# A feature-map attention block beside a Mish MLP on one core: a new order of all steps, first loads split anew over two queues, numerators over 64 rows

## The chip, the cores and the metric

One core of a Trainium2 chip. The time is that of one execution of the whole program on the device, in microseconds, lower is better. The kernel before took 151.50, 151.67 and 151.73 us in three runs, median 151.67.

## The reference, cut to what matters

All inputs are bf16; S = 2048 tokens, D = 448, 16 heads of 28, F = 1792.

```python
xn  = layernorm(x)                                # (1, 2048, 448)
q, k, v = heads(xn @ wqkv)                        # 16 heads of 28
phi(t) = concat(softmax(t @ w_phi), softmax(-(t @ w_phi)))   # per head, 56 wide
kv  = phi(k)^T @ v ;  z = sum over tokens of phi(k)
o   = (phi(q) @ kv) / (phi(q) @ z + 1e-6)
out = x + o @ wo + mish(xn @ w1 + b1) @ w2
```

## The kernel before, in words

The 2048 tokens are 16 tiles t of 128 and 8 units u of two tiles. Everything stays in SBUF; products go to the eight PSUM banks, which are taken in pairs. The program is a list of steps by name (`ORDER`). Each step issues instructions to one or more engines, and every engine works off its own instructions in the order of the list, waiting on semaphores only. So the list sets the order of all five engines and of both DMA queues (SP's and ACT's), and also which pair of banks a step gets: the pair that has lain unused longest.

The steps, by name (a last letter d, a, p, s or m says DVE, ACT, POOL, SP's queue or a transposing DMA; A, B, E, O, H are parts of a product over the 448 input rows):

- `lx6.8` loads tiles 6 and 7 of x. `lkm`, `lvm`: the first 384 rows of the key and value weights (tile `Wkv`). `lkt`: their last 64 rows, twice, "the tails". `lp`: w_phi into `Wbd`, four small loads. `lqT0` to `lqT3`: the query weights by transposing DMAs (`WqT`, L312). `lb`: b1. `l1m`, `l1t`, `l2.0` to `l2.3`, `lo`: W1, W2, wo.
- `zN`: N products of zeros, 128 by 512, whose result nobody reads (L406).
- `st`, `rs` or `rp`, `xn`: mean and variance of a tile, its reciprocal deviation, the normalized tile. `xtUm` transposes a unit of it by a DMA on SP's queue; `xt3E`, `xt3O` do it for unit 3 on PE (L514).
- `wtk0`, `wtk1`: PE transposes the key weights (L548), a copy goes to `Eq`. `wmk0`, `wmk1`: PE multiplies them by `Wbd` (L572), the copy is `Wpk`. `qd`: DVE doubles the last rows of `WqT` (L316). `wmq0`, `wmq1`: the same product for the query weights, the copy is `Wpq`.
- `kU`, `qU`, `vU`: the products of a unit of xn with `Wpk`, `Wpq` and the value weights, 14 products over 64 rows each (parts A, B, H) or 6 over 128 rows and 2 over 64 (E, O, H). When the last part is done, ACT takes two exponentials of k or q (L613, L679), and ACT or DVE copies v (L519, L521). All the products of these steps and of `f` are on line L441.
- `kn`: DVE sums and inverts (L621, L623), and POOL or DVE multiplies (L625). `kvU`: PE adds the unit to the one sum over tokens (L643). `kvz` writes it out and transposes it by a DMA into `KVZ`.
- `eT`: transposing DMA of the exponentials of q, tile t (`EqT`).
- `fQ.C`: the first MLP product for half Q of the tokens and chunk C of F; ACT applies Mish (L698).
- `ndT`: numerators and denominators of tile t, 16 products over 56 rows (L721), then six DVE instructions. `otU`: transposing DMA of the result.
- `gT`, `woU`: the second MLP product and the product with wo (L825, L842), added in one bank; DVE adds x (L790); `sto`, `stt` store. The last tile is stored in two parts, on ACT's and SP's queue.

Of the kernel before, what the change touches and what calls it, by code (L numbers as in the profile page):

```python
# [14 lines left out]
DH = 28  # L15
# [5 lines left out]
G = 4  # L21
# [17 lines left out]
class Program:  # L39
# [13 lines left out]
    def op(self, eng, fn, r=(), w=(), dma=False, tag="", after=()):  # L53
        o = Op()
        o.tag, o.parts = tag, None
        o.eng, o.fn, o.dma, o.needed, o.count, o.sem = eng, fn, dma, False, 0, None
        o.idx = len(self.ops[eng])
        deps = list(after)
        for res in list(r) + list(w):
            if res[0] == "ps":  # L60
                deps += [a for e, a in self.psum.get(res, {}).items() if e != eng]
        for res in r:
            if res[0] != "ps":
                deps += self.writers.get(res, [])
# [74 lines left out]
class Banks:  # L139
# [37 lines left out]


ORDER = """
zero pwd lkms lx6.8a table z14 ph lx4.6s pv lkta lpa st7d st4a st6d lx2.4s st5d pi pe wtk0d rp6p pp2 rp4p xn7a lbs lqT0 xn6d lqT2 b1 wtk1a  # L180
st2d xt3Ed lqT1 xn4d xt3Od lqT3 wmk0a xn5d wmk1a pp0 pk qd st3d v3Ha rp2p lvms wmq0d lx8.12s xn2d wmq1a st9a xn3d lx0.2s st11d v3Aa xt2m k3A
q3H st10d lx12.16s q3A st8d st0d rp10p xt1m rp8p st14d pp1 v3Ba q3B xn9d k3B v2Ha st15d xn10d xn8d st1d v2Aa q2B k3H v2Ba xn11d st13d q2H
rp14p rp0p k2B q2A l1ts k2A v1Bd xn14d xn15d st12d k2H k1H rp12p v1Ad k1B e6 xt4m v1Hd q1B ep k1A xt5m xt7m q1A k4B q1H v4Aa xn12d v4Ha k4A
xn13d k4H k5H xt6m k5A v4Ba xn0d e7 k5B xn1d xt0m e2 v5Ad l1ms v5Hd k7H kn2.1p kn1.0p k7A kn4.1p v5Bd kn4.0p k7B kn7.0p kn3.1p kn5.1p k6H
kn1.1p k6A q6B k6B q6H k0A q6A k0H v6Ha v6Aa k0B e3 q4B v6Ba v7Ba e5 q4A v7Ha v7Aa kn5.0p v0Ad e12 e4 e13 v0Hd kn7.1p kn3.0p f0.2H q4H v0Bd
f0.2B f0.3B f0.2A f0.3H f0.0A kn6.1p f0.0H f0.3A kn6.0p kn0.0p q5H f0.0B q0B q5A e8 kv4 kv1 f0.7H q5B f0.7A q0A kn2.0d q0H f0.7B kv5 kv7 kv6
f1.12H f1.12A f1.7A kn0.1d f1.12B f1.7B kv2 kv3 kv0 f0.12B e11 kvz e1 f1.11H f1.11A f1.7H f0.12A f0.12H f1.11B f0.8A f1.0B l2.0s f0.6B f0.9B
e9 f0.6A f1.0H f0.6H f0.8H f1.0A f0.9H f0.9A f0.10A f0.8B e10 f0.10B nd3 f0.10H f0.13B f1.10A f1.10H f0.13A f0.13H l2.3s f1.10B nd4 q7B
f1.8B q7A q7H f1.5B nd7 f1.8A f1.8H f1.5H f1.5A l2.2s f1.1H f1.1A los e0 f1.3A f1.1B f1.3B f1.9B nd1 f1.3H f1.9H f1.9A f0.11B f0.1A nd2
f0.1H f1.13A f0.1B f1.13B f0.11H f1.6H f1.13H f0.11A nd5 f1.6A f0.4H l2.1a e15 e14 f0.4A f1.6B f0.5B wob nd0 f0.4B f1.4B f0.5A f0.5H f1.2B  # L190
f1.4H ot1m f1.4A wo1H nd6 f1.2H f1.2A wo1B ot2m ot0m ot3m nd12 wo1A nd10 nd15 g3 g0 g2 g1 nd9 wo3B nd8 wo3H wo0B wo3A wo0H wo0A ot4m nd14 g6
g8 g7 wo4H ot7m wo2B nd13 sto0 wo4A nd11 sto3 wo4B g5 g9 g4 g10 ot5m ot6m wo5H wo7B wo5A wo6A wo2H wo2A wo7A wo7H wo6H wo5B wo6B sto1 g14
sto2 g11 g13 g12 sto4 sto6 stt14 sto5 g15 stt15
"""


# [5 lines left out]
def _kernel(es, nc, A_x, A_wqkv, A_w_phi, A_wo, B_w1, B_b1, B_w2, out):  # L202
    def sb(name, shape, dtype):
        return es.enter_context(nc.sbuf_tensor(name, shape, dtype))
# [37 lines left out]
    EqT = sb("EqT", [P, NT, 2 * G, P], BF16)  # L242
# [3 lines left out]
    KVZ = sb("KVZ", [P, 2 * G, P], BF16)  # L246
# [33 lines left out]
    def bank(b, n=1):  # L280
        return PS[:, b * TCW:(b + n) * TCW]
# [10 lines left out]
    def pb(b):  # L292
        return ("ps", b)
# [122 lines left out]
    def pe(fn, r, w, tag, after=()):  # L416
        return op("PE", fn, r=r, w=w, tag=tag, after=after)
# [295 lines left out]
    def nd(t):  # L713
        b = take2(False)

        def f(e):
            for s in range(2):
                for g in range(G):
                    for r in range(2):
                        at = (s * G + g) * NDW  # L720
                        ins = e.matmul(  # L721
                            bank(b + r)[:, at:at + NDW], EqT[64 * r:64 * r + QP, t, s * G + g, :],
                            KVZ[64 * r:64 * r + QP, 2 * g + s, 64 * r:64 * r + 64].rearrange("p (b c) -> p b c", b=2)[:, :, 0:DH + 2],
                            start=True, stop=True)
# [260 lines left out]
```

## Time and profile before

| What | Value |
|---|---|
| median of three runs | 151.67 us (151.50 to 151.73) |
| the profiled execution | 151.33 us, of which 149.0 us are span |
| busy in the span | PE 144.7, DVE 102.3, ACT 77.1, POOL 34.1 us |
| the fourteen zero products (L406) | 0.88 to 6.96 us |
| PE without a gap | from 12.00 to 146.07 us |
| one `st` step on ACT (L472, L474, L476) | 0.58 + 0.19 + 0.20 + 0.67 + 0.19 = 1.83 us |
| granted TensorE clock | 1.00 in all stages |

The span begins with the first instruction of the program and ends with the last; 2.33 us of the execution lie outside it. A row of the trace reads: start in us, length in us, engine, line, operation, what it writes and reads. A small q after an engine's name (SPq, ACTq) marks the issue of a transfer, and the time is that of the issue; the landing comes later. Matmuls overlap, so the distance between starts is what counts for them.

### The profile page before, as it was taken

The page shows a single profiled execution, that of the slowest core. Times are in us where ns is not written, and L with a number is a line of the kernel's source. Part 1 is how long each engine was busy: PE and PEld are TensorE (multiplying, and loading weights), DVE is VectorE, ACT ScalarE, POOL GpSimd, SP SyncE. Part 2 cuts the span into 40 slices and gives each one's busy share as a digit, 9 for nine tenths or more (in the row PEclk, how much of TensorE's full clock was granted, in tenths as well). Part 3 has the DMA queues.
Part 4 walks back from the last instruction along what each step waited for, and adds up shares of the span by engine and source line. Part 5 has one row for each costly group of instructions (what it writes and reads, how often), then busy time and mean ns, then how long its engine had stood idle before and what let it go on. Part 6 is the DMA issues. An engine that isn't in the chain of part 4 may idle for free.

```text
span 149.0 us, 3836 instructions
## 1 busy us (share of the span) xinstructions
PE 144.7 (97%) x1664; PEld 77.0 (52%) x1664; DVE 102.3 (69%) x214; ACT 77.1 (52%) x90; POOL 34.1 (23%) x46
## 2 busy tenths in 40 slices
PE   7979999999999999999999999999999999999993
PEld 2456555555445554445555556555554555665552
DVE  0699799999999940048939897997998891041222
ACT  3389999999899969587995776000000000000000
POOL 3233552599999900000000000000000000000000
PEclk9999999999999999999999999999999999999999
DMA  4999985689993305999250392200011507020005
GB/s 102 285 198 313 191 165 128 141 163 298 211 175 78 75 4 115 205 288 235 60 122 0 75 176 66 62 0 0 7 37 39 174 0 185 0 105 22 0 1 183
DMA packets 40980, 17.46 MB, mean 117 GB/s; under 512 B 34948, under 2 KB 40196, under 8 KB 40964
## 3 DMA queue, kind: packets, MB, share of 16 engines
q1 hardware_dynamic: 39484, 16.18, 49.4%
q10 hardware_dynamic: 1480, 1.04, 3.5%
q8 instruction: 13, 0.21, 0.6%
q14 instruction: 3, 0.02, 0.0%
HBM read 7.02 MB, written 1.84 MB: 59 GB/s over the span
## 4 chain that ended last, share of the span: by engine, by line
PE 96%; ACT 1%; DVE 1%; issue 0%; POOL 0%; POOLq 0%
PE PS L441 50%; PE PS L825 28%; PE PS L842 7%; PE PS L406 4%; PE PS L721 2%; PE PS L643 2%; PE PS L572 1%; ACT xn L504 1%; ACT Eq L519 1%; DVE Eq L521 0%; DVE x_all L790 0%; PE PS L548 0%; DVE x_all L811 0%; POOL zeros L363 0%; DVE shift L499 0%
## 5 line engine op out<-in xcount | busy, mean ns | idle before, releaser
L441 PE MATMUL PS<-xnT,W 64*128 64x512 bf16 x392 | 45.4, 376 | 0.0
L825 PE MATMUL PS<-W,actT 128*128 128x448 bf16 (+1 forms) x224 | 42.7, 351 | 0.0
L698 ACT ACTIVATE actT<-PS,b1T 128x1024 bf16<-128x1024 f32 x28 | 29.7, 1114 | 7.4 <-PE PS L441 7.4
L825 PEld LDWEIGHTS PS<-W,actT 128*128 128x128 bf16 x224 | 21.6, 98 | 20.2 <-issue 0.7
L441 PEld LDWEIGHTS PS<-xnT,W 64*128 64x128 bf16 x392 | 19.4, 94 | 20.0 <-ACT actT L698 0.8
L625 POOL TENSOR_TENSOR actT<-actT,rSk 128x896 bf16<-128x896 bf16 x14 | 24.1, 1760 | 3.3 <-DVE rSk L623 3.3
L790 DVE TENSOR_TENSOR x_all<-PS,x_all 128x448 bf16<-128x448 f32 (+1 forms) x16 | 9.6, 617 | 19.0 <-PE PS L825 11.3
L621 DVE TENSOR_REDUCE Sk<-actT 128x32 f32<-128x896 bf16 x16 | 16.6, 1039 | 0.0
L613 ACT ACTIVATE actT<-PS 128x896 bf16<-128x896 f32 x16 | 14.0, 941 | 0.5 <-PE PS L441 0.2
L441 PE MATMUL PS<-Wpq,xnT 64*128 64x448 bf16 x112 | 14.0, 349 | 0.0
L441 PE MATMUL PS<-Wpk,xnT 64*128 64x448 bf16 x112 | 13.5, 349 | 0.0
L441 PE MATMUL PS<-Wkv,xnT 64*128 64x448 bf16 x112 | 13.3, 350 | 0.0
L737 DVE COPY Sq<-PS 128x32 f32<-128x32 f32 x16 | 3.0, 188 | 14.8 <-PE PS L721 14.8
L480 DVE BATCH_NORM_STATS2 stats<-x_all 128x6 f32<-128x448 bf16 x14 | 8.6, 614 | 3.9 <-DMA x_all<-in_A_x_dram 3.9
L746 DVE TENSOR_TENSOR v_all<-v_all 128x464 f32<-128x464 f32 x16 | 10.3, 642 | 0.6
L742 DVE TENSOR_TENSOR v_all<-PS,Sq 128x464 f32<-128x464 f32 x16 | 10.3, 642 | 0.6
L750 DVE TENSOR_TENSOR xn<-v_all,rden 128x448 bf16<-128x448 f32 x16 | 10.0, 624 | 0.6
L744 DVE TENSOR_TENSOR v_all<-PS,Sq 128x464 f32<-128x464 f32 x16 | 10.1, 631 | 0.0
L679 ACT ACTIVATE actT<-PS 128x896 bf16<-128x896 f32 x10 | 8.7, 923 | 0.4 <-DMA EqT<-actT 0.4
L441 PEld LDWEIGHTS PS<-Wpk,xnT 64*128 64x128 bf16 x112 | 5.8, 94 | 4.8
L441 PEld LDWEIGHTS PS<-Wpq,xnT 64*128 64x128 bf16 x112 | 5.7, 94 | 4.8 <-DVE Wpq L521 0.3
L441 PEld LDWEIGHTS PS<-Wkv,xnT 64*128 64x128 bf16 x112 | 5.5, 94 | 5.1 <-DVE v_all L521 0.4
(77 smaller groups left out, 121.8 us busy)
## 6 DMA issues: line engine op xcount, KB each, us to landing
out_dram<-x_all SPq DMA_DIRECT2D x7, 224.0 KB, 2.1
W<-in_B_w_dram SPq DMA_DIRECT2D x1, 1344.0 KB, 7.6
x_all<-in_A_x_dram SPq DMA_DIRECT2D x2, 448.0 KB, 4.8
Wkv<-in_A_wqkv_dram SPq DMA_DIRECT2D x2, 336.0 KB, 4.2
x_all<-in_A_x_dram SPq DMA_DIRECT2D x3, 224.0 KB, 4.7
W<-in_B_w_dram SPq DMA_DIRECT2D x2, 336.0 KB, 4.0
Wo<-in_A_wo_dram SPq DMA_DIRECT2D x2, 336.0 KB, 6.2
W<-in_B_w_dram SPq DMA_DIRECT2D x2, 224.0 KB, 4.5
```

The source lines that it names most:

```text
L441: ins = e.matmul(o, lhs(c, k), rhs(c, k), start=par in first and n == at[par][0], stop=par in last and n == at[par][-1])
L613: op("ACT", lambda e, s=s: e.activation(E_of(u)[:, s, :, :], two(b, D), ACT.Exp, scale=1.0 if s == 0 else -1.0), r=[pb(b), pb(b + 1)], w=[ ...
L621: op("DVE", lambda e: e.tensor_reduce(Sk[u][:, s, :], Eh(), AX.X, ALU.add), r=[("E", u, s)], w=[("Sk", u, s)], tag=f"Sk{u}.{s}")
L625: op(eng, lambda e: e.tensor_tensor(Eh(), Eh(), ap_on(rSk[u][:, s, 0:1], [[1, 2 * H], [0, DH]]), ALU.mult), r=[("E", u, s), ("rSk", u, s)] ...
L698: op("ACT", lambda e: e.activation(actT[:, fc, q * 1024:(q + 1) * 1024], bank(b, 2), ACT.Mish, bias=b1T[:, fc:fc + 1]), r=[("b1T",), pb(b) ...
L742: op("DVE", lambda e: e.tensor_tensor(tv(t1), num(0), sx(1), ALU.mult), r=[pb(b), pb(b + 1), ("Sq", i)], w=[("t1", i)], tag=f"ta{t}")
L744: op("DVE", lambda e: e.tensor_tensor(tv(t2), num(1), sx(0), ALU.mult), r=[pb(b), pb(b + 1), ("Sq", i)], w=[("t2", i)], tag=f"tb{t}")
L746: op("DVE", lambda e: e.tensor_tensor(t1, t1, t2, ALU.add), r=[("t1", i), ("t2", i)], w=[("t1", i)], tag=f"tc{t}")
L750: op("DVE", lambda e: e.tensor_tensor(o_sb[k][:, t % 2, :].rearrange("p (h d) -> p h d", d=DH), t1[:, :, 0:DH], ap_on(rden[i][:, 0:1], [[1 ...
L790: op("DVE", lambda e: e.tensor_tensor(x_all[:, t, 0:n], bank(b)[:, 0:n], x_all[:, t, 0:n], ALU.add), r=[pb(b), ("x", t)], w=[("out", t)], ...
L825: ins = e.matmul(bank(b)[:, 0:width(t)], actT[:, fc, tok(t)], W2[:, fc, 0:width(t)], start=first and fc == 0, stop=last and fc == FC - 1)
L842: ins = e.matmul(bank(b)[:, 0:w], oT_of(u)[lo:hi, cc * P:(cc + 1) * P], Wo[lo:hi, cc, 0:w], start=first and n == at[par][0], stop=last and ...
```

## The change

The list `ORDER` is written anew, from its first step to its last, and the numerators multiply over all 64 rows of a half (the eight added rows hold zeros in both operands) instead of 56. The heads of the two lists and the other edit:

```diff
 ORDER = """
-zero pwd lkms lx6.8a table z14 ph lx4.6s pv lkta lpa st7d st4a st6d lx2.4s st5d pi pe wtk0d rp6p pp2 rp4p xn7a lbs lqT0 xn6d lqT2 b1 wtk1a
-st2d xt3Ed lqT1 xn4d xt3Od lqT3 wmk0a xn5d wmk1a pp0 pk qd st3d v3Ha rp2p lvms wmq0d lx8.12s xn2d wmq1a st9a xn3d lx0.2s st11d v3Aa xt2m k3A
...
+zero pwd lkma lx6.8s lkta lps pv lqT3 pi pe ph pp0 st7d lx4.6a z10 lqT0 pk table st6d lx2.4a lvma rs7a rs6a lqT1 lqT2 xn7d wtk0b xn6d wtk1a
+st5d st4d xt3Oa xt3Ea lx8.12s z4 rp4a st2d wmk1a xn5d wmk0a v3Ha xn4d qd v3Oa st3d v3Ea rp2p wmq0d wmq1a st9d xn2d k3O xn3d k3E lbs st8d b1
...
-                            bank(b + r)[:, at:at + NDW], EqT[64 * r:64 * r + QP, t, s * G + g, :],
-                            KVZ[64 * r:64 * r + QP, 2 * g + s, 64 * r:64 * r + 64].rearrange("p (b c) -> p b c", b=2)[:, :, 0:DH + 2],
+                            bank(b + r)[:, at:at + NDW], EqT[64 * r:64 * r + 64, t, s * G + g, :],
+                            KVZ[64 * r:64 * r + 64, 2 * g + s, 64 * r:64 * r + 64].rearrange("p (b c) -> p b c", b=2)[:, :, 0:DH + 2],
```

The steps are the same but for who does them. The zero products are 10 and later 4, instead of 14. To ACT's queue go the key weights, x tiles 4 to 5 and 2 to 3, and the value weights; to SP's queue x tiles 6 to 7 and w_phi. Tile 7 is normalized by DVE instead of ACT, tile 9 by ACT instead of DVE. The statistics of tiles 4 and 9 go from ACT to DVE, the reciprocal deviations of tiles 4 to 7 from POOL to ACT, the copies of xt3 and half of that of wtk0 from DVE to ACT. v1 and v5 are copied by ACT, v6 by DVE. Units 3 (k, q, v), 2 and 1 (v), and 1 (k) use parts E and O. `kn` on DVE is now that of 5.0 and 3.0 instead of 2.0 and 0.1. W2's last part is loaded on ACT's queue instead of its second.

On PE, in the head of the program, before:

```order
L406 MATMUL PS<-zeros 128x512 x14
L548 MATMUL PS<-ident,Wkv 112x128 x8
L692 MATMUL PS<-ident,b_rows 128x14
L548 MATMUL PS<-ident,Wkv 112x128 x8
L514 MATMUL PS<-ident,xn 128x128 x7
L572 MATMUL PS<-Wbd,Eq 128x112 x16
L441 MATMUL PS<-Wkv,xnT 128x448 x2
L572 MATMUL PS<-Wbd,WqT 128x112 x16
L441 MATMUL PS<-Wkv,xnT 128x448 x6
L441 MATMUL PS<-Wpk,xnT 128x448 x6
```

and after:

```order
L406 MATMUL PS<-zeros 128x512 x10
L548 MATMUL PS<-ident,Wkv 112x128 x16
L514 MATMUL PS<-ident,xn 128x128 x7
L406 MATMUL PS<-zeros 128x512 x4
L572 MATMUL PS<-Wbd,Eq 128x112 x16
L441 MATMUL PS<-Wkv,xnT 128x448 x8
L572 MATMUL PS<-Wbd,WqT 128x112 x16
L441 MATMUL PS<-Wpk,xnT 128x448 x6
L692 MATMUL PS<-ident,b_rows 128x14
L441 MATMUL PS<-Wpk,xnT 128x448 x2
```

Four zero products moved behind the transposition of x (L514). All of `v3` (eight products over `Wkv`) now stands ahead of the products over `WqT`, where before only its part H did. The small product for b1 moved from between the weight transpositions to the last part of `k3`.

On SP's queue, its first entries, before:

```order
L303 DMA Wkv<-in_A_wqkv_dram 128x3x448
L300 DMA x_all<-in_A_x_dram 128x896 x2
L337 DMA b_rows<-in_B_b_dram 14x128
L312 DMA_TRANSPOSE WqT<-in_A_wqkv_dram 128x448 x4
L303 DMA Wkv<-in_A_wqkv_dram 128x3x448
L300 DMA x_all<-in_A_x_dram 128x1792
L300 DMA x_all<-in_A_x_dram 128x896
L525 DMA_TRANSPOSE xnT<-xn 128x7x128
```

and after:

```order
L300 DMA x_all<-in_A_x_dram 128x896
L329 DMA Wbd<-in_A_w_phi_dram 28x4x28 x4
L312 DMA_TRANSPOSE WqT<-in_A_wqkv_dram 128x448 x4
L300 DMA x_all<-in_A_x_dram 128x1792
L337 DMA b_rows<-in_B_b_dram 14x128
L300 DMA x_all<-in_A_x_dram 128x1792
L525 DMA_TRANSPOSE xnT<-xn 128x7x128
```

Both weight loads (`Wkv`) and two loads of x left the queue, w_phi (`Wbd`) came ahead of the transposing loads of `WqT`, and b1 moved behind them and behind x tiles 8 to 11.

On ACT, its first instructions, before:

```order
L300 DMA x_all<-in_A_x_dram 128x896
L357 ACT_TABLE_LOAD
L308 DMA Wkv<-in_A_wqkv_dram 64x896 x2
L329 DMA Wbd<-in_A_w_phi_dram 28x4x28 x4
L472 ACTIVATE junk,mv<-x_all 128x448
L474 ACTIVATE rmean<-mv 128x1
```

and after:

```order
L303 DMA Wkv<-in_A_wqkv_dram 128x3x448
L308 DMA Wkv<-in_A_wqkv_dram 64x896 x2
L300 DMA x_all<-in_A_x_dram 128x896
L357 ACT_TABLE_LOAD
L300 DMA x_all<-in_A_x_dram 128x896
L303 DMA Wkv<-in_A_wqkv_dram 128x3x448
L491 ACTIVATE lnv<-mv,eps_col 128x1
```

ACT issues the key weights first, then the tails, two loads of x and, sixth, the value weights; then come the short steps of the reciprocal deviation (L491, L493) where the statistics of tile 4 stood.

More of the change, by code (lines that the diff above doesn't have):

```diff
@@ L179 @@
 ORDER = """
-zero pwd lkms lx6.8a table z14 ph lx4.6s pv lkta lpa st7d st4a st6d lx2.4s st5d pi pe wtk0d rp6p pp2 rp4p xn7a lbs lqT0 xn6d lqT2 b1 wtk1a
-st2d xt3Ed lqT1 xn4d xt3Od lqT3 wmk0a xn5d wmk1a pp0 pk qd st3d v3Ha rp2p lvms wmq0d lx8.12s xn2d wmq1a st9a xn3d lx0.2s st11d v3Aa xt2m k3A
-q3H st10d lx12.16s q3A st8d st0d rp10p xt1m rp8p st14d pp1 v3Ba q3B xn9d k3B v2Ha st15d xn10d xn8d st1d v2Aa q2B k3H v2Ba xn11d st13d q2H
-rp14p rp0p k2B q2A l1ts k2A v1Bd xn14d xn15d st12d k2H k1H rp12p v1Ad k1B e6 xt4m v1Hd q1B ep k1A xt5m xt7m q1A k4B q1H v4Aa xn12d v4Ha k4A
@@ L184 @@
[L184 to L191, printed above, removed]
@@ L192 @@
-g8 g7 wo4H ot7m wo2B nd13 sto0 wo4A nd11 sto3 wo4B g5 g9 g4 g10 ot5m ot6m wo5H wo7B wo5A wo6A wo2H wo2A wo7A wo7H wo6H wo5B wo6B sto1 g14
-sto2 g11 g13 g12 sto4 sto6 stt14 sto5 g15 stt15
+zero pwd lkma lx6.8s lkta lps pv lqT3 pi pe ph pp0 st7d lx4.6a z10 lqT0 pk table st6d lx2.4a lvma rs7a rs6a lqT1 lqT2 xn7d wtk0b xn6d wtk1a
+st5d st4d xt3Oa xt3Ea lx8.12s z4 rp4a st2d wmk1a xn5d wmk0a v3Ha xn4d qd v3Oa st3d v3Ea rp2p wmq0d wmq1a st9d xn2d k3O xn3d k3E lbs st8d b1
+lx12.16s st14d xt2m st15d l1ts xt1m k3H q3O pp2 q3E rp8p lx0.2s q3H rp14p k2A k2H xn9a q2H xn8d q2A st13d st12d rp12p k2B xn15d st10d xt4m
@@ new lines @@
+xn12d q2B xn13d v2Ha v2Ea v2Oa v1Oa st11d k1O st1d v1Ea st0d k1E v1Ha rp10p xn10d xn14d pp1 ep k1H k4B rp0p q1A e7 k4H xt6m k4A xn0d v4Ha
+xn1d q1B v4Aa e6 q1H k6H xt7m xn11d k6A v4Ba kn1.1p v6Ad kn2.0p k6B kn4.1p v6Hd xt0m q6A xt5m q6H l1ms v6Bd q6B k7H k7A k0B kn6.1p k7B k0H
+kn1.0p k0A v5Aa kn6.0p v5Ha v7Aa k5A k5H v7Ha v5Ba k5B q4B v7Ba kn0.0p e2 e3 kn4.0p kn0.1p kn2.1p q4A f0.3B e13 e5 e4 q4H f0.2H f0.2A f0.3H
+f0.0A f0.3A f0.0H v0Ad e12 kn7.0p kn7.1p v0Hd f0.2B v0Bd f0.0B kn3.1p q5H q5A kn5.1p los kn5.0d kn3.0d q0H q0A q5B kv6 kv4 kv0 kv2 kv1 q0B
@@ new lines @@
+f1.7A f1.7H f0.6H f0.6A f1.7B wob f1.12H f1.12A f0.6B f1.12B f0.9A kv5 kv3 kv7 f0.9H e9 kvz f0.13B f0.9B f1.11B f0.13A f1.11A f1.11H f0.10B
+f0.13H f0.7B f0.10H f0.10A f1.10B l2.3a f0.12B f0.7A f0.7H f1.10H nd6 e8 f1.10A f0.12A f0.8H f0.12H f0.8A nd7 f1.0B e1 l2.1s e11 e0 f0.8B
+f1.0H f1.0A q7B nd2 f1.2H q7A q7H f1.2B f1.8B f1.2A f1.8H f1.1H f1.8A f1.1A f0.11A f0.11H f1.1B l2.0s f1.6B f0.11B f1.6H nd4 f1.6A ot3m
+f0.5A f1.9B e15 e10 e14 f0.5B nd5 l2.2s f0.4A f0.5H f1.9A f1.9H f0.4H f1.3A nd1 f1.3H f0.4B f1.5B f1.3B f0.1H nd0 f1.5H f0.1B f1.5A f0.1A
@@ L194 @@
+ot2m ot0m f1.4H f1.4A f1.13B f1.4B wo3A nd3 f1.13A wo3B nd8 wo3H f1.13H ot1m nd11 g6 g2 g7 wo0H nd13 wo0A nd14 wo1B wo0B nd10 wo1A wo1H g0
+g3 g1 wo2B nd12 wo2H nd15 wo2A ot6m ot5m ot7m nd9 g5 g4 g13 g12 ot4m g10 wo4A wo5H wo7A wo6H wo4B wo5A wo7H wo6B wo5B wo7B wo4H wo6A sto1 g8
+g9 g11 sto2 g14 sto0 sto4 sto5 stt14 sto3 g15 sto6 stt15
 """
```

## The prediction

> **What bounds the kernel now.** I read the page's first part, then busy time by stage, then the chain that ended last.
>
> ```profile
> span 149.0 us, 3836 instructions
> PE 144.7 (97%) x1664; PEld 77.0 (52%) x1664; DVE 102.3 (69%) x214; ACT 77.1 (52%) x90; POOL 34.1 (23%) x46
> ```
> ```profile
> 12.00:54.00 42.00, 42.00 (x658) 22.33 (x658) 39.20 (x78) 40.81 (x50) 29.70 (x27) 1.00 0.80 164
> ```
> ```profile
> 0.88 6.08 PE PS L406 x14
> ...
> 7.45 0.69 DVE Eq L521
> ...
> 8.24 1.04 ACT xn L504 x2
> 9.28 0.92 ACT Eq L519
> ...
> 12.00 33.77 PE PS L441 x348
> ...
> 92.98 10.70 PE PS L825 x56
> ...
> 146.09 0.56 DVE x_all L790
> ```
> The second fence is one stage, 12 to 54 us: its length, then PE, PEld, DVE, ACT and POOL busy. PE has no gap in it, and the chain stays on PE from 12.00 to the last add at 146.09. So a new order of PE's steps after 12 us saves nothing by itself; it can only open gaps. What can shrink is the head (12.0 us) and the tail (2.9 us: last add, last store). In the head, PE works off zero products until 6.96; then the chain goes through a copy, ACT's normalizing of x, and another copy. And ACT is busy 40.81 of the 42.00 us of the long stage: whatever PE gains in the head, ACT must be able to follow.
>
> **The tail** keeps `g15` and tile 15's split store at its end, with the same products and adds. Only the stores issued just ahead are others (`sto3`, `sto6` for `sto4`, `sto6`, `sto5`): 0, bounds -0.1 and +0.1.
>
> **Numerators over 64 rows** instead of 56: 256 products whose added rows are zeros.
> ```profile
> L721 PEld LDWEIGHTS PS<-KVZ,EqT x256: 92/93/97, 64.6 to 116.8; 56*128 56x128 bf16 x128
> L441 PEld LDWEIGHTS PS<-Wpk,xnT 64*128 64x128 bf16 x112 | 5.8, 94 | 4.8
> ```
> A weight load of 56 rows takes 93 ns, one of 64 rows 94: 0, at worst 256 x 1 ns = 0.3 us. Whole-row products (parts E and O) now do for units 3, 2 and 1 what pairs of 64-row products (A and B) did: 10.70/56 = 191 ns for a whole-row product of 448 columns, 190 ns for a pair (below): 0.
>
> **The head, step by step**, in the clock of before.
> ```profile
> 4.38 0.63 DVE L480 BATCH_NORM_STATS2 stats<-x_all 128x6 f32<-128x448 bf16 x1 [3.25 <-DMA x_all<-in_A_x_dram]
> 5.04 0.18 DVE L481 BATCH_NORM_AGGREGATE mv<-stats 128x2 f32<-128x6 f32 x1
> 5.77 0.18 DVE L481 BATCH_NORM_AGGREGATE mv<-stats 128x2 f32<-128x6 f32 x1
> 6.69 0.20 ACT L474 ACTIVATE rmean<-mv 128x1 f32<-128x1 f32 x1
> 8.12 0.39 DVE L508 TENSOR_SCALAR xn<-x_all,mv,rstd 128x448 bf16<-128x448 bf16 x1
> 10.14 0.58 DVE L508 TENSOR_SCALAR xn<-x_all,mv,rstd 128x64 bf16<-128x64 bf16 x2
> 9.18 1.00 ACT L519 ACTIVATE Eq<-PS 112x1024 bf16<-112x1024 bf16 x1
> 10.16 1.73 ACT L519 ACTIVATE Wpk<-PS 128x896 bf16<-128x896 f32 x2
> ```
> *First x.* It stands first on SP's queue instead of ACT's, and the key weights the other way round. ACT's x let DVE start at 4.38, 3.6 us after its issue; SP's first load, half again as large, took 4.4 (row below). I take 4.38, from the load of the same size; bounds 0 and +0.8. The statistics of tiles 7 and 6 end at 5.22 and 5.95. Two short ACT steps per tile (0.20 each, some 0.5 a pair with the hand-over) take the place of POOL's. So DVE normalizes tile 7 from 5.95 (0.58), does half of the first weight copy (half of 0.69), then tile 6 (0.39): ready at 7.3, against 9.28 before, where ACT did tile 7.
>
> *Tails of the key weights* are ACT's second and third issue, as before; the second eight weight transpositions wait for them.
> ```profile
> L308 ACTq DMA_DIRECT2D Wkv<-in_A_wqkv_dram x2: 531/570/608, 1.2 to 1.8; - x2
> ...
> DMA to landing us min/median/max: 5.2/5.6/6.0
> ```
> That is 6.4 to 7.8. In the same queue they now follow a larger load, but no x runs on SP's queue beside them; I take the middle, 7.1, and keep both ends.
>
> *ACT's copies* come in its order: half a weight copy (until 7.0), the second weight copy (1.00, from 7.8), x's two transposed halves (some 1.0 together by the same row), a pair of short steps, the two `Wpk` copies (1.73): 8.8, 9.8, 10.3, 12.0. PE's `z4`, its 16 key products (0.9) and `v3H` fit in by 9.9. With the tails at 7.8 it all ends 0.7 later.
> ```profile
> 0.73 0.45 SPq L303 DMA_DIRECT2D Wkv<-in_A_wqkv_dram  x1
> 2.45 2.26 ACTq L329 DMA_DIRECT2D Wbd<-in_A_w_phi_dram  x4
> 2.75 5.12 SPq L312 DMA_TRANSPOSE WqT<-in_A_wqkv_dram  x4
> 7.92 0.59 SPq L303 DMA_DIRECT2D Wkv<-in_A_wqkv_dram  x1
> ...
> DMA to landing us min/median/max: 4.0/4.2/4.4
> ...
> 10.63 0.22 DVE L316 COPY WqT<-WqT 128x256 bf16<-128x256 bf16 x1
> 11.04 0.96 PE L572 MATMUL PS<-Wbd,WqT 112*128 112x112 bf16 x16
> 13.91 0.75 PE L441 MATMUL PS<-Wkv,xnT 64*128 64x448 bf16 x6
> 14.48 0.74 PE L441 MATMUL PS<-Wpq,xnT 64*128 64x448 bf16 x6
> ```
> *Value weights* left SP at 7.92, behind the four transposing loads (`WqT`). On ACT's queue five issues of about half a microsecond go ahead of them: issued near 3.5, and with the longest landing seen on that queue (6.0) there at 9.5. Bounds 7.5 (4.0 after issue) and 11.9 (7.92 + 4.0, the place of before, if sharing the transfer engines eats the whole lead). I take 9.5, which is hidden behind `v3H` at 9.9.
>
> *Transposing loads.* They started at 2.75, behind a weight load, two loads of x and b1. Now one x (0.5) and the four w_phi issues (2.26) stand ahead: 3.5, 0.75 later. DVE's doubling copy moves from 10.63 to 11.3 with them; at best it stays, since less data stands ahead in the queue. What is queued behind that copy on DVE (more statistics) waits for x anyway.
>
> *Gain.* The products over `WqT` start at 11.3 and end at 12.3, against 12.00. But by then `v3O` and `v3E` are done: six pairs, 9.9 to 11.1, which came after 12.00 before (six products in 14.48 - 13.91 = 0.57, so 1.14 in all). That is 1.14 - 0.3 = 0.8 us. Bounds: 1.1 with the doubling copy at its old time, and -0.9 with the value weights at 11.9 (v3 until 13.0, products until 14.0, against 12.00 + 1.14).
>
> *b1* moves behind 448 KB of x on SP's queue, and its small product now stands between `k3E` and `k3H`, wanted near 13.4; PE waits in order.
> ```profile
> x_all<-in_A_x_dram SPq DMA_DIRECT2D x2, 448.0 KB, 4.8
> ```
> The x ahead is issued near 8.7 and lands near 13.5 by this row, b1 right behind: 0 to 0.5. I take 0, since the value weights, which then stood ahead in that queue, are gone from it.
>
> **After the head.** ACT loses two statistics (1.8 each, the table above) and gains three pairs of short steps, half a weight copy, x's copies and one more v copy (0.9): even. In 12 to 54 us it idled 1.19, of which these two waits are 0.56:
> ```profile
> 32.58 1.73 ACT L613 ACTIVATE actT<-PS 128x896 bf16<-128x896 f32 x2 [0.17 <-PE PS L441]
> 39.74 1.73 ACT L679 ACTIVATE actT<-PS 128x896 bf16<-128x896 f32 x2 [0.39 <-DMA EqT<-actT]
> ```
> So ACT can follow a lead of some 1.2 - 0.56 = 0.6 us; beyond that PE waits for ACT to empty PSUM banks. So 0.8 becomes **0.6**. DVE's own last product for k ended at 52.8, for kv0; its list up to there is 0.5 shorter, and kv3, now last, is wanted near 52.5: hidden. POOL's run without a gap and start as much earlier:
> ```profile
> 27.75 24.09 POOL L625 TENSOR_TENSOR actT<-actT,rSk 128x896 bf16<-128x896 bf16 x14 [3.27 <-DVE rSk L623]
> 51.70 1.09 DVE L625 TENSOR_TENSOR actT<-actT,rSk 128x896 bf16<-128x896 bf16 x1
> ```
> If either is late, `kv5` or `kv3` stops PE by as much.
>
> **Sum.** The profiled execution took 151.33 us, 149.0 of it span: 151.33 - 0.6 = 150.7. The median of the runs, 151.67, lies 0.34 higher, so I forecast 151.1.
>
> **Rivals.** *PE stays slow* (ends on the other side). Ten zero products end near 5.2 us, not 6.96. In before each starts 0.43 after the last, though 448 columns later take 0.19; PE was quick from the weight transpositions on:
> ```profile
> 5.55 0.15 PEld L406 LDWEIGHTS PS<-zeros 128*128 128x128 bf16 x1 [0.28 <-issue]
> 5.98 0.15 PEld L406 LDWEIGHTS PS<-zeros 128*128 128x128 bf16 x1 [0.28 <-issue]
> ...
> 6.80 0.61 PE L548 MATMUL PS<-ident,Wkv 128*112 128x128 bf16 x8
> ```
> So PE changed speed after 6.4, at least 5.5 us after its first product; the granted clock reads 1.00 throughout and does not show it. If ten are too few, all that follows takes double until PE has been busy long enough: `z4` 1.7 instead of 0.85, the key products +0.9, v3 +1.3, the query products +0.9. The break-even, with 0.6 lost, is PE slow until about 11; slow until 13.5 costs some 2 us. That makes 151.4 to 153.7, in the middle 152.7. For it: 5.5 us were needed, and now there are 4.3, then pauses for tails and x. Against: transpositions and `z4` follow within 3 us. Chance 0.2.
> [...]
>
> *The lead is lost*, to loads that collide (tails or value weights near their late ends), to b1, or to ACT: no change, 151.4 to 151.9. For: ACT's 97% of its stage. Against: the value weights have over 2 us to their late end. Chance 0.23.
>
> *A new wait inside the stream*: at `kv3`, at q4's buffers (the 0.39 above; W1's main load is now issued ahead of both transfers that free them), or at numerators that follow each other more closely than DVE empties their banks. With 0.5 to 1.5 us over before, 152.2 to 153.2. Chance 0.05.
>
> **How the numbers follow.** The forecast's own range is 150.5 to 151.4, its chance 0.52. No change means within 0.2%, 0.3 us, about what a measurement can tell. So faster 0.52, same 0.23, slower 0.25. The range 150.4 to 152.9 takes in the best end (1.1 kept whole) and the better part of the slow case.
>
> **What would show it.** Right: the first products over `Wkv` and `xnT` in a run of eight before 11.2, those over `WqT` ended near 12.3, no 0.43 spacing after 7 us, the last add near 145.5. Wrong: `z4` spaced 0.43 and sixteen `WqT` products in 1.7 us; `v3O` waiting for `Wkv`; or PE idle between 20 and 55 us.

## The result, and the profile after

The changed kernel took 149.90 us (median of seven runs, 149.50 to 150.82) against 151.60 for the kernel before in the same comparison. The ratio is 0.9898, with a 95% interval of 0.9865 to 0.9932; the two medians alone give 0.9888. The forecast was 151.1, with a range that began at 150.4.

Over all the comparisons below, 124 executions of the kernel before had a median of 151.28 us with a span of 149.05, and 27 of the changed kernel, the seven above among them, 150.06 with 148.2. Five disturbed executions, of 215 to 847 us, count in none of the ratios. So the span lost 0.85 us, and what lies outside it went from a mean of 2.21 to 1.93 us: 0.28. The mean granted clock of an execution is given where it matters: 1.00 in all 27 of the changed kernel and in all but 3 of the 124.

The profiled execution of the changed kernel is the slowest of its seven (150.82). Its page, its stage from 12 to 54 us and its chain, in the columns shown of before:

```profile
span 148.9 us, 3768 instructions
PE 143.3 (96%) x1628; PEld 74.6 (50%) x1628; DVE 101.0 (68%) x215; ACT 77.3 (52%) x90; POOL 33.2 (22%) x42
```
```profile
12.00:54.00 42.00, 42.00 (x546) 21.46 (x545) 39.14 (x82) 40.64 (x48) 31.32 (x30) 1.00 0.83 179
```
```profile
3.55 7.24 DMA Wkv<-in_A_wqkv_dram
...
10.84 1.31 PE PS L441 x6
12.15 0.96 PE PS L572 x16
...
145.92 0.56 DVE x_all L790
```

The stage is as full as before: PE 42.00 of 42.00, ACT 40.64. The chain no longer runs through DVE and ACT into PE's products (L572), but from ACT's sixth issue, the value weights, straight to PE, and stays there to the last add. Rows of the head in the same execution (start, length, what it waited for):

```profile
3.72 0.63 DVE L480 BATCH_NORM_STATS2 stats<-x_all 128x6 f32<-128x448 bf16 x1 [2.60 <-DMA x_all<-in_A_x_dram]
...
7.04 0.65 PE L548 MATMUL PS<-ident,Wkv 128*112 128x128 bf16 x8 [1.25 <-DMA Wkv<-in_A_wqkv_dram]
7.92 1.03 PE L406 MATMUL PS<-zeros 128*128 128x512 bf16 x4
10.84 1.31 PE L441 MATMUL PS<-Wkv,xnT 128*128 128x448 bf16 x6 [0.78 <-DMA Wkv<-in_A_wqkv_dram]
11.87 0.23 DVE L316 COPY WqT<-WqT 128x256 bf16<-128x256 bf16 x1 [0.90 <-DMA WqT<-in_A_wqkv_dram]
12.15 0.96 PE L572 MATMUL PS<-Wbd,WqT 112*128 112x112 bf16 x16
```

x arrives 0.66 us earlier than before (3.72 against 4.38), the four later zeros run at twice the speed of the first (1.03 for four; they start 0.22 apart, the first 0.43), and then the value weights come at 10.8 and the last part of `WqT` just ahead of 11.87. In this execution the products over `WqT` start 1.1 us later than before (11.04), but all of `v3` is done. That leaves a last add at 145.92 against 146.09: 0.17 us. The median gain does not show in this trace. A better one is that of `a_w56` below, the changed kernel but for rows of zeros that cost nothing (187 ns a product with and without them), and in which PE, behind a wait of 0.54 for the tails, waited for no load by more than about 0.2 us:

```profile
9.10 1.82 PE L441 MATMUL PS<-Wkv,xnT 64*128 64x448 bf16 x8
10.87 0.96 PE L572 MATMUL PS<-Wbd,WqT 112*128 112x112 bf16 x16
...
14.74 0.92 PE L441 MATMUL PS<-Wpk,xnT 64*128 64x448 bf16 x8
...
144.68 0.56 DVE L790 TENSOR_TENSOR x_all<-PS,x_all 128x384 bf16<-128x384 f32 x1 [1.65 <-PE PS L825]
```

Here PE goes through `v3` without a wait that the trace lists (its chain still has the load of the value weights in it, 4.1% of the span; the six whole-row products begin at 9.10 + 1.82 - 1.31 = 9.61). The products over `WqT` start at 10.87, `k2` at 14.74, and the last add stands at 144.68, 1.41 earlier than before. In ten traces, three of the changed kernel and seven of variants that leave the order behind the head alone, the last add comes 129.9 to 130.1 us after the first product of `k2` (144.68 - 14.74 = 129.94). a_vlastz below, with zeros added in the head, took longer: 133.4 from there to the end of its span (16.07 to 149.5), against 132.9 in a_w56 (14.74 to 147.6). So among these kernels the head alone sets the time, and the head differs from execution to execution by when its loads land (the value weights at 9.4 to 10.8).

Against before, the rest is no shorter either. Before took 135.05 us from its first product over `WqT` (11.04) to its last add (146.09), and in that time PE also did `v3O` and `v3E`, 1.14 us by the distance of their starts: 133.91 are left. a_w56 took 133.81 (10.87 to 144.68).

### The profile page after: what moved, and what is told of

The parts are those of the page before. It is cut to its first block, busy times and chain, and to the rows that moved or that the text cites. A ratio compares the mean times of both kernels' runs of the same rounds, so it can differ in the third digit from the quotient of the medians.

```text
span 148.9 us, 3768 instructions
## 1 busy us (share of the span) xinstructions
PE 143.3 (96%) x1628; PEld 74.6 (50%) x1628; DVE 101.0 (68%) x215; ACT 77.3 (52%) x90; POOL 33.2 (22%) x42
## 3 DMA queue, kind: packets, MB, share of 16 engines
q10 hardware_dynamic: 1920, 1.93, 5.8%
## 4 chain that ended last, share of the span: by engine, by line
PE 91%; DMA 5%; ACTq 1%; DVE 1%; ACT 0%; issue 0%
PE PS L441 50%; PE PS L825 29%; PE PS L842 7%; DMA Wkv<-in_A_wqkv_dram 5%; PE PS L721 2%; PE PS L643 2%; ACTq L308 1%; PE PS L572 1%; ACTq L300 0%; DVE x_all L790 0%; ACTq L303 0%; ACT L357 0%; DVE x_all L811 0%; PE PS L692 0%
## 5 line engine op out<-in xcount | busy, mean ns | idle before, releaser
L441 PEld LDWEIGHTS PS<-xnT,W 64*128 64x128 bf16 x392 | 18.5, 94 | 20.8 <-ACT actT L698 0.9
L441 PE MATMUL PS<-Wkv,xnT 64*128 64x448 bf16 (+1 forms) x94 | 13.2, 350 | 0.8 <-DMA Wkv<-in_A_wqkv_dram 0.8
L441 PE MATMUL PS<-Wpq,xnT 64*128 64x448 bf16 (+1 forms) x106 | 13.2, 350 | 0.0
L441 PE MATMUL PS<-Wpk,xnT 64*128 64x448 bf16 (+1 forms) x100 | 12.7, 350 | 0.0
L480 DVE BATCH_NORM_STATS2 stats<-x_all 128x6 f32<-128x448 bf16 x16 | 9.7, 609 | 3.6 <-DMA x_all<-in_A_x_dram 3.6
L744 DVE TENSOR_TENSOR v_all<-PS,Sq 128x464 f32<-128x464 f32 x16 | 10.1, 629 | 0.0
L441 PEld LDWEIGHTS PS<-Wkv,xnT 64*128 64x128 bf16 (+1 forms) x94 | 5.4, 95 | 6.5 <-DMA Wkv<-in_A_wqkv_dram 1.0
L441 PEld LDWEIGHTS PS<-Wpq,xnT 64*128 64x128 bf16 (+1 forms) x106 | 5.4, 94 | 5.2 <-issue 0.4
L441 PEld LDWEIGHTS PS<-Wpk,xnT 64*128 64x128 bf16 (+1 forms) x100 | 5.3, 94 | 4.8 <-issue 0.2
```

The costliest lines, as they stand in the source:

```text
L441: ins = e.matmul(o, lhs(c, k), rhs(c, k), start=par in first and n == at[par][0], stop=par in last and n == at[par][-1])
L480: op("DVE", lambda e: e.bn_stats(stats[:, t, :], x_all[:, t, :]), r=[("x", t)], w=[("st", t)], tag=f"bn{t}")
```

## The experiments

Theories: **HEAD** (the gain is a shorter head, by new places of loads and of v3's products), against **REST** (it lies behind the head), **ZEROS** (four zero products fewer) and **OUTSIDE** (outside the span). Each kernel ran in five rounds beside the kernel before, whose median was between 151.18 and 151.41. The two ran on several chips, so kernels are best compared by their ratios.

**The changed kernel again** (x_after, x_after2, x_after3; no edit).

> The changed kernel again, unaltered, for the trace of another execution. The profiled one took 150.82 us, 0.9 over the median of its runs. Theory HEAD (the 1.7 us come from a shorter head, which the profiled execution had lost to value weights that landed late, at 10.79): here the value weights land before 10, the products over WqT end before 12.2 and the last add stands near 145.0. Theory REST (the gain lies behind the head): the head ends near 13.1 as in the profiled execution, and what is shorter lies behind it. Theory OUTSIDE (time outside the span): the span is as long as before's, 149, and the time outside it near 1.0. All three: 149.9 us, ratio 0.989.

> The changed kernel, unaltered. HEAD: 149.9 us, ratio 0.989 to 0.991; value weights landed before 10.2, the products over WqT from 10.8 to 11.4, the last add at 144.9 to 145.4, before's being at 146.09.

> The changed kernel, unaltered, once more. If the difference of 0.4 us to the kernel with 56 rows was a late load on that chip: 149.8 to 150.1 us, within 0.15 of the kernel with 56 rows beside it. If 64 rows cost it: again 0.3 to 0.5 above.

Measured: 149.99 us (ratio 0.9875, interval 0.9829 to 0.9920), 150.33 (0.9937, 0.9915 to 0.9958) and 149.78 (0.9907, 0.9874 to 0.9939). Of the first there is no trace. That of the second shows a wait that the prediction had not named, for the transposed x of unit 2:

```profile
9.09 1.68 PE L441 MATMUL PS<-Wkv,xnT 64*128 64x448 bf16 x8
10.74 0.96 PE L572 MATMUL PS<-Wbd,WqT 112*128 112x112 bf16 x16
...
15.60 0.93 PE L441 MATMUL PS<-Wpk,xnT 64*128 64x448 bf16 x8 [0.82 <-DMA xnT<-xn]
...
145.63 0.56 DVE L790 TENSOR_TENSOR x_all<-PS,x_all 128x384 bf16<-128x384 f32 x1 [1.65 <-PE PS L825]
```

So the lead is there (10.74), and 0.82 of it goes to a transfer that was issued at 9.88 and took 5.7 us, behind 448 KB of x tiles 8 to 11 and as much of 12 to 15 on SP's queue. HEAD's last adds, 144.9 to 145.4, were missed by the two traces of x_after2 and x_after3 (145.63 and 145.61). The spans of all 27 executions, 0.85 shorter, would put the median one near 145.2, which no trace shows. The same kernel on the same chip gave 150.33 and 149.78, so differences of half a microsecond between two comparisons mean little. OUTSIDE has 0.28 us and not more.

**headafter**: the changed kernel's list up to `q3H`, then before's.

```diff
-... lx0.2s q3H rp14p k2A k2H xn9a q2H xn8d q2A st13d st12d ...
+... lx0.2s q3H st11d st10d st0d rp10p pp1 xn9d v2Ha xn10d xn8d st1d ...
```

> The changed kernel's list up to the step q3H and its numerators over 64 rows; behind that the list of before in its own order. HEAD: the whole gain, 149.7 to 150.2 us. REST: no gain, 151.4 to 151.9. In between both have a part, and this run gives the head's.

Measured: 153.17 us, 1.0112 (1.0078 to 1.0147): slower. The head was as early as any (products over `WqT` at 11.65), but PE then stood still inside the stream. Its waits from 20 to 60 us:

```profile
PE PS L441 <- DMA xnT<-xn: 0.9, 1, 0.9
PE PS L441 <- DVE v_all L521: 0.8, 1, 0.8
PE PS L441 <- ACT actT L679: 0.3, 1, 0.3
PE PS L441 <- ACT actT L698: 0.2, 1, 0.2
```

None of the theories had this in its numbers, HEAD's 149.7 to 150.2 included. The early head was worth nothing with a list behind it that makes PE wait 2.2 us for a transfer, for DVE and for ACT.

**a_oldhead**: the changed kernel with before's loads, zeros and order on PE put back in the head.

```diff
-zero pwd lkma lx6.8s lkta lps ... lx4.6a z10 ... lx2.4a lvma ... z4 ... v3Ha xn4d qd v3Oa st3d v3Ea rp2p wmq0d wmq1a
+zero pwd lkms lx6.8a table z14 ph lx4.6s pv lkta lpa ... lx2.4s ... lbs ... b1 ... v3Ha xn4d qd st3d rp2p lvms wmq0d wmq1a lx8.12s v3Oa v3Ea
```

> The changed kernel with the head of before put back in its place: key weights, x tiles 4 to 5 and 2 to 3, b1, then the transposing loads, then the value weights on SP's queue; x tiles 6 to 7, tails and w_phi on ACT's; fourteen zeros at the start; the products over WqT ahead of v3O and v3E. What the engines copy, and all that follows, is the changed kernel's. Theory HEAD: the gain goes, 150.9 to 151.6 us. Theory REST: it stays, 149.8 to 150.2. Where the list behind it is made for an earlier head (as the list of before was not able to use one), it may come out worse than before, 151.6 to 153.

Measured: 152.29 us, 1.0051 (1.0015 to 1.0086). With the granted clock at 1.00 (seven of twelve executions) the median is 152.02. So all of the gain goes and 0.7 more, and REST falls. The number is that of the expectation's last case, but not its reason. In the trace PE is busy for all of the 70 us from 20 to 90. Its products for `q3` start at 17.44, 2.86 later than in the first trace of the changed kernel (14.58), and its span is 2.8 longer (151.7 against 148.9). The loss is all in the head, where the products over `WqT` start at 12.39 (before: 11.04), and in this execution a low granted clock follows (0.57 from 12 to 16 us). So in this trace the mixed head is slower than that of either kernel.

**a_wvs, a_vlast, a_swap**: one part of the head undone in each.

```diff
# a_wvs: value weights behind the transposing loads on SP's queue
-... lx2.4a lvma rs7a ... xt3Ea lx8.12s z4 ...
+... lx2.4a rs7a ... xt3Ea lvms lx8.12s z4 ...
# a_vlast: v3O and v3E behind the products over WqT
-... qd v3Oa st3d v3Ea rp2p wmq0d wmq1a st9d xn2d k3O ...
+... qd st3d rp2p wmq0d wmq1a st9d xn2d v3Oa v3Ea k3O ...
# a_swap: first loads exchanged
-zero pwd lkma lx6.8s ...
+zero pwd lkms lx6.8a ...
```

> The changed kernel with one load moved: the value weights on SP's queue behind the transposing loads, as in before, instead of ACT's. They then land near 12 instead of 9.4 to 10.8. Theory HEAD, with the value weights as its main part: v3O waits until 12, PE is 1.2 to 2.5 us later, 151.1 to 152.4 us. Rival (ACT and the loads behind set the pace, so a lead on PE is not kept): 149.9 to 150.4.

> The changed kernel with v3O and v3E behind the products over WqT on PE, as in before. Theory HEAD: PE has nothing to do between v3H and the doubling copy (9.3 to 10.8 in the execution whose value weights landed at 9.41), so 1.1 us go, 150.8 to 151.2 us. Rival (the lead is lost later anyway): 149.8 to 150.2.

> The changed kernel with the first two loads exchanged as in before: key weights first on SP's queue, x tiles 6 to 7 first on ACT's. x lands 0.5 to 0.7 us later, the key weights at the same time. If x sets the pace of the head (normalizing, transposing, then v3H): 150.3 to 150.7 us. If the value weights and WqT do, which land at 9.4 to 10.8: 149.8 to 150.1.

Measured: a_wvs 153.17 us, 1.0091 (1.0056 to 1.0126). a_vlast 151.37, 1.0015 (0.9980 to 1.0051). a_swap 149.98, 0.9896 (0.9865 to 0.9928). Both of the first two came in two groups. At a mean granted clock of 1.00, a_wvs took 151.6 (three executions) and a_vlast 150.98 (seven); at 0.989, in one execution 0.978, 153.2 (nine) and 152.7 (five). One of a_swap's six was at 0.989 too (153.03). What PE waited for in a_wvs, in a_vlast, and in a_swap:

```profile
11.84 1.31 PE L441 MATMUL PS<-Wkv,xnT 128*128 128x448 bf16 x6 [2.45 <-DMA Wkv<-in_A_wqkv_dram]
```
```profile
10.79 0.96 PE L572 MATMUL PS<-Wbd,WqT 112*128 112x112 bf16 x16 [1.68 <-DVE WqT L316]
11.59 2.17 PE L441 MATMUL PS<-Wkv,xnT 128*128 128x448 bf16 x6
```
```profile
10.02 1.31 PE L441 MATMUL PS<-Wkv,xnT 128*128 128x448 bf16 x6 [0.44 <-DMA Wkv<-in_A_wqkv_dram]
```

By the executions at 1.00, undoing the value weights' queue costs 1.5 us against the 150.06 of the changed kernel, and undoing the place of `v3O` and `v3E` 0.9. The whole gain is 1.2, so each loses all or most of it: the two need each other, as far as three executions of a_wvs can tell. The exchange of the first two loads is worth nothing: x landed at 4.1 us instead of 3.6 to 4.0, and the value weights still come last.

**b_z10, b_z10z8, a_vlastz, a_z14, a_noz4, a_noz4b**: the zeros.

```diff
# b_z10: before, ten zero products instead of fourteen
-... table z14 ph ...
+... table z10 ph ...
# b_z10z8: the same, and eight more ahead of b1
-... lqT2 b1 wtk1a ...
+... lqT2 z8 b1 wtk1a ...
# a_vlastz: a_vlast with eight zero products in PE's pause
-... rp2p wmq0d ...
+... rp2p z8 wmq0d ...
# a_z14: changed kernel, fourteen at the start, none later
-... z10 ... z4 ...
+... z14 ...
# a_noz4 and a_noz4b (the same kernel twice): changed kernel without the later four
-... lx8.12s z4 rp4a ...
+... lx8.12s rp4a ...
```

> The kernel before with ten zero products in place of fourteen, nothing else. Theory ZEROS (four zero products of 0.43 us each hold PE up until 6.96 in before, though its weights have landed by then, and the gain is that they are gone): 150.0 to 150.6 us. Rival HEAD (the weights, x and WqT set the head's pace, PE waits for them at 12.00 with or without zeros): 151.4 to 151.9. Rival SLOW PE (ten are too few to bring PE to its fast state before its real work starts): 152.0 to 153.5.

> The kernel before with ten zero products at the start instead of fourteen, and eight more in the gap between the first weight transposition and b1, where PE idled 1.9 us in b_z10 (152.3 us, clock 0.977 to 0.989 in all its executions, 0.52 and 0.63 from 10 to 14 us). PAUSE: the low clock goes and with it 1.0 us, 151.0 to 151.5, clock 1.00. Rival TOO FEW (ten at the start are too few, whatever comes later): 152.0 to 152.6.

> As a_vlast (v3O and v3E behind the products over WqT), with eight more zero products on PE behind v3H, where PE otherwise idles 1.7 us for WqT. They fit in that gap. Theory PAUSE (a PE that idles for over some 1.5 us falls to half speed for about 3 us, in part of the executions; a_vlast came at 150.7 to 151.5 us with a mean granted clock of 1.00 and at 152.2 to 153.2 with 0.989): the upper group goes, all executions at 1.00 and 150.7 to 151.3 us. Rival (the upper group has another cause, the loads for instance): both groups stay, median 151.2 to 152.3.

> The changed kernel with fourteen zero products at the start and none behind the transposition of x. ZEROS: the gain goes back by what four zero products take, 0.8 to 1.7 us, so 150.7 to 151.6. HEAD: PE has time until the value weights land, so 149.8 to 150.2. SLOW PE: faster than the changed kernel by 0.1 to 0.5, since it comes to its fast state before the weight transpositions in every execution.

> The changed kernel without the four zero products behind the transposition of x. PE then has its pauses for data (0.4 to 1.3 us each) bare. PAUSE: no pause reaches 1.5 us in most executions, so 149.7 to 150.1, with perhaps one in four executions at 0.989 and 151.5. Rival (PE has to be kept busy without a gap until the real stream): most executions near 151.5, median 151 to 152.

> The changed kernel without the four later zeros, a second time, beside the changed kernel on the same chip. If these zeros keep PE fast: again 151 or more, executions at a granted clock below 1.00 or a slow stretch in the head, last add after 146. If the first result was the late landing of stores that one trace shows (3.6 to 3.9 us instead of 1.6): near 150.0 to 150.4, last add near 145.2.

Measured: b_z10 152.36 us, 1.0055 (1.0021 to 1.0090), all twelve executions at 0.977 to 0.989. b_z10z8 151.38, 0.9997 (0.9977 to 1.0017), all twelve at 1.00. a_vlastz 151.19, 0.9987 (0.9966 to 1.0008), all twelve at 0.999 or 1.00. ZEROS falls: fewer zeros in before make it slower. SLOW PE's number came (152.0 to 153.5), but b_z10z8, also with ten at the start, took its 1.0 us back by filling a later pause. The stages of b_z10, then of b_z10z8 (length, PE busy, PEld, DVE, ACT, POOL, granted clock):

```profile
6.60:10.00 3.40, 1.61 (x24) 1.37 (x24) 2.69 (x10) 2.92 (x6) 1.46 (x4) 1.00 1.14 144
10.00:13.50 3.50, 3.50 (x33) 2.51 (x32) 2.68 (x9) 2.18 (x3) 1.57 (x4) 0.51 1.09 344
```
```profile
6.60:10.00 3.40, 2.81 (x27) 1.63 (x26) 2.90 (x11) 3.15 (x8) 1.67 (x4) 1.00 1.39 147
10.00:13.50 3.50, 3.50 (x50) 2.29 (x49) 3.44 (x11) 3.15 (x7) 1.60 (x4) 1.00 1.07 333
```

And those of a_vlast, then of a_vlastz:

```profile
8.40:11.80 3.40, 1.72 (x29) 1.27 (x27) 2.69 (x9) 2.13 (x6) 0.22 (x1) 1.00 1.14 263
11.80:15.20 3.40, 3.40 (x11) 1.45 (x10) 3.05 (x9) 1.88 (x3) 0.96 (x4) 0.51 1.17 275
```
```profile
8.40:11.80 3.40, 3.24 (x38) 2.15 (x37) 2.66 (x10) 2.54 (x6) 0.08 (x1) 1.00 1.15 280
11.80:15.20 3.40, 3.40 (x23) 1.63 (x21) 3.33 (x11) 2.35 (x4) 1.00 (x3) 1.00 1.11 293
```

In these traces PE is busy for 1.61 or 1.72 of 3.40 us, and the next 3.4 run at half clock. By windows of half a microsecond the low clock lasts 3.41 us in b_z10 (0.58 in the one from 10.0, 0.50 in five, 0.51 in the one from 13.0) and 3.42 in a_vlast, so the stretch ahead of it is taken as long. The same stretch filled to 2.81 or 3.24 was followed by 1.00. Half clock for 3.4 us is 1.7 us of PE's work. The groups of a_wvs and a_vlast lie 1.6 and 1.7 apart, b_z10 and b_z10z8 1.0.

The busy share of the stretch alone does not tell when the clock falls, though. Two more, of a_oldhead just ahead of its fall and of a_wvs:

```profile
8.87:12.27 3.40, 1.70 (x26) 1.17 (x23) 2.66 (x11) 3.28 (x7) 0.00 (x0) 1.00 0.97 301
```
```profile
9.00:12.40 3.40, 0.95 (x7) 0.41 (x6) 1.82 (x7) 1.95 (x4) 1.04 (x3) 1.00 0.90 260
```

In a_oldhead no single pause in the stretch was longer than 1.1 us, and the clock fell at about 12.3. In this execution of a_wvs PE was busy for 0.95 us only, with a wait of 2.45 in the stretch, and the clock stayed at 1.00; nine others of the same kernel have the lower mean. What decides between them is not shown. In both pairs zeros in PE's pause came with a clock of 1.00 in all twelve executions; the kernel before, with fourteen at the start, had it in all but 3 of 124.

a_z14: 150.10 us, 0.9887 (0.9845 to 0.9930), so fourteen at the start do as well as ten and four. a_noz4: 151.35, 0.9998 (0.9965 to 1.0032); a_noz4b, on the chip of x_after2 (150.33): 151.22, 0.9998 (0.9971 to 1.0026). So without the later four it is 0.9 us slower on the same chip, as the expectation's rival had it, but how is not shown. A bare pause behind the transposition of x is not enough, since a_z14 has one as well (0.49 us, against 0.68 and 0.69). Only one of the 24 executions was at 0.989, the rest at 0.995 and above, and the last adds of both traces are early (145.21 and 145.46). In the first trace, what is longer lies behind the last add, where a store took up to 4.2 us to land. The first line is from it, the second from the changed kernel's first profile (columns: shortest, middle, longest):

```profile
DMA to landing us min/median/max: 1.9/2.2/4.2
```
```profile
DMA to landing us min/median/max: 1.9/2.2/2.6
```

In the second trace 2.7 us lie outside the span (151.10 - 148.4), not 2.0. Neither has an evident tie to four zeros at 8 us. Over all 24 executions the time outside the span is 2.0 us against 1.93, and the spans are 1.1 to 1.2 longer (149.4 and 149.25 against 148.2), so the loss lies inside the span of executions that were not traced. That PE stayed slow longer there, with ten zeros in all, is not excluded: the granted clock reads 1.00 over the slow zeros at the start too (ten from 0.88 to 5.12 in the first trace). This is open.

**a_w56 and a_w56b**: the numerators back to 56 rows.

```diff
-EqT[64 * r:64 * r + 64, t, s * G + g, :], KVZ[64 * r:64 * r + 64, ...
+EqT[64 * r:64 * r + QP, t, s * G + g, :], KVZ[64 * r:64 * r + QP, ...
```

> The changed kernel with the numerators over 56 rows again. If the edit costs nothing (a weight load of 56 rows took 93 ns, one of 64 rows 94): 149.8 to 150.1 us, as the changed kernel beside it. If rows or the pairing with their neighbours count: 150.3 or more (the edit has a share in the gain), or 149.6 and less.

> The changed kernel with the numerators over 56 rows, once more. If 64 rows cost 0.4 us: 149.5 to 149.9, with 0.3 to 0.5 to the changed kernel beside it, and a shorter stretch between the first product of k2 and the last add. If they cost nothing: within 0.15 of it, and that stretch equal within 0.1 (it was 129.94 with 56 rows, 130.03 with 64).

Measured: 149.92 us, 0.9909 (0.9880 to 0.9937), beside x_after2's 150.33; then 150.34, 0.9920 (0.9887 to 0.9954), beside x_after3's 149.78. Once 0.4 faster, once 0.6 slower: the edit has no effect that shows. Its products with 64 rows (x_after2), then with 56 (a_w56):

```profile
L721 PE MATMUL PS<-KVZ,EqT x256: 187/187/188, 63.1 to 113.8; 64*128 64x60 bf16 x128
```
```profile
L721 PE MATMUL PS<-KVZ,EqT x256: 185/187/190, 62.1 to 112.8; 56*128 56x60 bf16 x128
```

**a_xt2 and a_wv1**: two tries at a faster one.

```diff
# a_xt2: unit 2 of x transposed ahead of the load of tiles 12 to 15
-... b1 lx12.16s st14d xt2m st15d ...
+... b1 xt2m lx12.16s st14d st15d ...
# a_wv1: value weights ahead of x tiles 2 to 3, st2 later
-... st6d lx2.4a lvma ... rp4a st2d wmk1a ... xn4d qd ...
+... st6d lvma lx2.4a ... rp4a wmk1a ... xn4d st2d qd ...
```

> The changed kernel with the transposing load of x unit 2 ahead of the load of x tiles 12 to 15 on SP's queue (448 KB). In one execution PE waited 0.46 us for that unit at 15.27, in two others not at all. If the lead of the head is limited there: 149.5 to 149.8 us. If not, or if tiles 12 to 15 then come too late for their statistics: 149.9 to 150.5.

> The changed kernel with the value weights ahead of x tiles 2 to 3 on ACT's queue, and the statistics of tile 2 behind the normalizing of tile 4. If the landing of the value weights sets the head's pace: they land 0.3 to 0.6 us earlier, 149.4 to 149.7 us. If WqT does, which lands at about the same time: 149.8 to 150.0. If x tiles 2 to 3 come too late: 150.2 to 151.

Measured: a_xt2 150.74 us, 0.9956 (0.9929 to 0.9983), above all four ratios of the changed kernel, though its interval overlaps that of x_after2. a_wv1 150.17, 0.9928 (0.9905 to 0.9952), no better. In a_xt2 unit 2 came in time, but the next unit did not (its chain):

```profile
14.52 5.17 DMA xnT<-xn
19.69 0.14 issue
19.83 26.75 PE PS L441 x262
```

In a_wv1 the value weights were there when `v3` came to them, and it ran without a wait (eight products in 1.60 us from 9.22 on), but then `WqT` was last:

```profile
11.52 0.96 PE L572 MATMUL PS<-Wbd,WqT 112*128 112x112 bf16 x16 [0.69 <-DVE WqT L316]
```

No variant was clearly faster than the changed kernel. In both tries, a load brought forward made another one late.

## Why the prediction was wrong

The sign held, and so did the main mechanism, a shorter head. The size did not: the forecast gain was 0.6 us, and the measured one 1.2 over all executions (151.28 to 150.06) and 1.7 in the first comparison. Three terms failed: the 0.6 that ACT was to let through, the time outside the span, which was put at no change, and the scale of 151.67. By the prediction's own steps:

*Sum and scale.* "The median of the runs, 151.67, lies 0.34 higher" was the largest single error, 0.39. The three runs were high; over 124 executions the median is 151.28, and the profiled execution (151.33) was a typical one. Without this step the forecast is 150.7, inside the executions of the changed kernel (149.5 to 150.8). In the first comparison, before's median was as high (151.60); there all of the miss is in the gain.

*Outside the span.* The sum took 2.33 us as given, without a reason. It was 2.21 in the mean of before and 1.93 in that of after, 0.28 that had no step. headafter, with only the new head, had 2.06, and a_oldhead, with only the new rest, 2.02; what sets it is not known.

*After the head: "0.8 becomes 0.6".* Wrong in its mechanism. A full lead of 1.41 us (a_w56) went through to the end; ACT was busy 40.73 of 42 us there and PE never waited for it:

```profile
12.00:54.00 42.00, 42.00 (x629) 21.50 (x628) 38.10 (x80) 40.73 (x48) 31.02 (x29) 1.00 0.82 172
```

I had taken two waits of ACT (0.56) out of its idle time as if a new order had to keep them.

*Gain of the head: 0.8.* The right size for the median (the span lost 0.85), but partly by luck, since several of its terms were others. First x: 3.72, not 4.38, which moved nothing (a_swap). x ready at 7.3: the last normalizing began at 6.24 and took 0.39, so 6.6. Tails: the second weight transposition began at 7.04 in the first trace and between 5.9 and 6.6 in most others, forecast 7.1. Value weights: 9.4 in x_after2 (where the six whole-row products begin at 9.09 + 1.68 - 1.31 = 9.46), 10.1 in x_after3 and 10.8 in the first trace, forecast 9.5; PE waited for them in part of the executions only. Products over `WqT`: 10.74 to 12.15, forecast 11.3. The best end, "1.1 with the doubling copy at its old time", was too near: 1.41 was seen. The wait for x's unit 2 (0.16 to 0.82 us in four of seven traces) stood in no step. *b1* at 0 was right, as were the tail, the numerators and whole rows against pairs.

*Rivals.* "PE stays slow" did not come in the changed kernel: PE reached its full speed between 4.3 and 6 us in the three traces (the first eight weight transpositions took 0.62 us in the first and 0.96 in x_after3, the next eight 0.65 in both; in x_after2 all sixteen took 1.45), and no low clock was granted in 27 executions. But its price was right in kind. In b_z10 the trigger was not "ten are too few" by itself: PE had reached full speed (eight weight transpositions in 0.65 at 8.27) and fell again, behind a stretch in which it was busy about half the time (1.61 of 3.40). For a_noz4, with ten in all, "too few" is not excluded. "The lead is lost" describes the first profile (0.17 left), by late value weights, but not the median. "A new wait inside the stream" came in headafter (over 2 us), not in the changed kernel.

The range was too high at its lower end, since it took the scale of 151.67 and 1.1 as the most that the head could give.

## What to carry to other kernels

Where PE is full behind the head, find in the trace which transfers the head waits for, place early work that needs none of the late ones in the gap, and look at several executions: one trace cannot tell which load is the late one. Move the head and the list behind it together, since either alone lost time here (153.17 and 152.29 us). Where a trace shows PE pausing for half of a stretch of a few microseconds (busy for 1.61 to 1.72 of 3.40 in three traces here), look for executions with a lower mean granted clock, and try to fill the pauses with products that nobody reads. Pauses of 1.7 to 2.5 us here cost another 1.0 to 1.7 us in part or all of the executions; one of 1.25 in the first trace of the changed kernel cost only itself, but two of 0.7 and 1.1 close together in a_oldhead did not.

## What was not expected of the hardware

The granted clock reads 1.00 over the zeros at the start, which run at half speed (0.43 us from start to start, 0.22 for later ones), but does show the later fall: 0.50 to 0.51 for 3.4 us, after 3.4 us with PE busy for 47 to 51 percent (1.61, 1.70 and 1.72 of 3.40), and no fall at 83 percent (2.81). Yet one execution of a_wvs kept 1.00 over a stretch that was busy for 28 percent (0.95). The same loads of the same kernel landed up to 1.4 us apart between executions (value weights 9.4 and 10.8), and two programs that differ in little but their order had 2.21 and 1.93 us outside the span.
